# Attention beside a long convolution on one core: contiguous taps in the Toeplitz tiles, a ring of 15 exponential tiles, a shared pool of two PSUM banks, and an order that counts TensorE's changes of shape

## The chip, the cores and the metric

One NeuronCore of a Trainium2 chip (trn2). The metric is device time in microseconds (us) of one execution; lower is better.

## What is computed

The output is `g * a + (1 - g) * b` for 2048 positions and 448 channels, in bfloat16. `a` is attention with 16 query heads of 28 channels that share one key and one value head; `b` is a state-space layer, that is a causal convolution of every channel with 2048 taps of its own; `g` is one gate per position.

```python
g = sigmoid((x * gate_w).sum(-1, keepdims=True))
# a: attention
q = x @ wq                       # 16 heads of 28
k, v = x @ wk, x @ wv            # one head
p = softmax(q k^T * 28 ** -0.5)  # 16 x 2048 x 2048
a = (p v) @ wo
# b: state-space layer; A, B, C are complex, 448 x 256 states
K[d, l] = Re(sum_n C[d,n] * exp(dt[d] * A[d,n] * l) * dt[d] * B[d,n])   # l = 0..2047
y[d, t] = sum_l K[d, l] * x[t - l, d]
b = y + x * Dskip
```

## The kernel before

**A recorded program and a planner.** The kernel does not write its instruction streams by hand. Every piece of work is recorded with `Prog.op` or `Prog.dma`: its engine, the time the author assumes for it in ns, the names it reads and writes, and a priority `pr` (lower goes first). `Prog.schedule` is a list scheduler: it keeps a clock per engine, takes again and again the ready operation that can start earliest (then the lowest priority), and so fixes the order of all five engines. `Prog.emit` writes that order with semaphore waits. On the chip each engine follows its list strictly; an instruction whose input is late holds up everything behind it on that engine. The planner's constants (60 ns from one engine to another, 300 ns per DMA issue, 2200 ns from a DMA's end to its use) move nothing by themselves, but they decide the order.

**Attention.** The scores are cut into 1024 tiles of 128 keys by 512 queries: 16 groups (four query chunks times four groups of four heads) of 64 tiles each. I call such a group a head group, or head for short; its index is `i`. `qk(s)` in `main()` (L988) computes a set of alternately three and two tiles into five PSUM banks (0 to 2 and 3 to 4 of `psS`); each tile uses 29 rows of the array, so tiles of four heads lie in four row strips. One ScalarE instruction (L1001) turns the set into exponentials in `expT`, a ring of ten tiles. `pv(v)` (L1010) multiplies four tiles with `vaug` (values, and a column of ones for the denominator) into `psB`, in four column strips of 32. The lines that set the ring and its order are

```python
es = ts[0] % 10                                  # L1000, in qk(s)
... wr=[("e", t % 10) for t in ts] ...           # L1002
... rd=["va"] + [("e", t % 10) for t in ts] ...  # L1014, in pv(v)
qk(s)                                            # the loop of main()
if s >= 2:
    while nv < NTL // 4 and 4 * nv + 3 <= sets[s - 2][-1]:
        pv(nv); nv += 1
```

`norm(i)` follows a head's last product: VectorE copies `psB` to `acc` (L910), four DMAs fetch the denominators (`denT`), VectorE takes the reciprocal (L915), two more steps of DMA spread it over the partitions through `R_scratch` (`rdenB`), and L919 scales the result. `qproj(i)` makes the queries of a later head (L663, L669, L672, L675), `outp` multiplies by `wo` (L893, L902).

**The convolution.** The 448 channels go in 14 blocks of 32 (index `c`). `masters(b)` (every two blocks) and `tables(c)` build powers of `exp(dt A)` on VectorE by repeated doubling (L698 to L796); one copy of the tables is in use while the next is built. `kgen(u)` takes 16 channels: 64 matmuls (L814) give their taps, VectorE copies them from PSUM to `kstg` with the channels interleaved (L824) and adds `Dskip` to tap 0 (L827), and one DMA writes 128 pieces of 512 bytes to `KP_scratch` in DRAM. There each group of four channels is one line in which the four channels alternate, element by element.

`tload(gi)` loads one Toeplitz tile for four channels: 128 partitions of 4096 elements (8192 bytes), each partition starting one tap later than the one before; the second 64 partitions begin 1024 taps further on. Four buffers (`NTR = 4`) take turns. `conv(c)` (16 channels, 28 calls, four tiles each) multiplies each tile with the input `U`, eight groups of four matmuls, one per channel and column strip:

```python
r = e.matmul(ps.v(32 * j, 32 - 2 * n, po + 128 * k, [[1, 128]]),              # L856
             self.U.v(0, P, (4 * gi + j) * 32 + 2 * n, [[1, 32 - 2 * n]]),
             self.T.v(0, P, s * 4096 + (896 - 128 * n) * 4 + j, [[4, 128]]), ...)
```

The moving operand is thus read with a step of four elements. VectorE scales the sum (`cst`, L865), TensorE turns it round (L876), and VectorE adds it to the output tile `O` (L884). The convolution has the lowest priority of all work for TensorE.

**PSUM.** Bank 5 belongs to the sums of `conv` alone (lock `"C"`). Bank 7 (`psX`) serves everything else in turn (lock `"X"`): `qproj`, `kgen`, the turning in `conv`, `outp`, and the transposes at the start.

**Queues.** All DMAs but five loads at the start are issued by SP, in the planner's order: T loads, taps, denominators and their spreading, and the output. `tail()` finishes the last head, folds and stores.

Of the kernel before, what the change touches and what calls it, by code (L numbers as in the profile page):

```python
# [11 lines left out]
P = 128  # L12

S = 2048
# [6 lines left out]
KPW = 2112  # L21
# [9 lines left out]
NTR = 4  # L31
SIN2PI = 6.2831850
# [19 lines left out]

def dram(t, off, dims):
    return bass.AP(tensor=t.tensor, offset=t.offset + off, ap=[list(d) for d in dims])


class Op:
    __slots__ = ("i", "eng", "fn", "ns", "lat", "deps", "pr", "lock", "unlock", "slot", "ndma",
                 "count", "vc", "end", "comm", "extra")


class Prog:
    SEM_NS = 60
    DMA_NS = 2200
    SLACK = {"pe": 500.0, "dve": 300.0}
# [9 lines left out]
    def op(self, eng, fn, ns, rd=(), wr=(), pr=0, lat=60, lock=None, unlock=None, comm=None):  # L75
        o = Op()
        o.i, o.eng, o.fn, o.ns, o.lat, o.pr = len(self.ops), eng, fn, ns, lat, pr
        o.lock, o.unlock, o.slot, o.ndma = lock, unlock, None, 0
        o.comm = comm
        deps = {}  # L80
# [40 lines left out]
    def schedule(self):  # L121
# [15 lines left out]
        locks = {}  # L137
# [3 lines left out]
        while done < n:  # L141
            best = None
            for e in ENG:
                T = free[e]
                for i in ready[e]:
                    o = ops[i]
                    r = max(rt[i], T)
                    if o.lock is not None:
                        L = locks.setdefault(o.lock, [None, 0.0, []])
                        if L[0] is not None:  # L150
                            continue
                        r = max(r, L[1])
# [9 lines left out]
            ready[e].remove(i)  # L162
            if e == "pool" and o.slot is None:
                for d in reversed(order[e]):
                    if ops[d].slot is None:
                        o.deps[d] = 1
                        break
# [5 lines left out]
            if o.lock is not None:  # L173
                L = locks[o.lock]
                for d in L[2]:
                    o.deps.setdefault(d, 1)
                L[0] = o.i
                L[2] = []
            if o.slot is not None:
                free[e] = r + 300.0 * o.ndma  # L180
# [7 lines left out]
            if o.unlock is not None:  # L188
                L = locks[o.unlock]
                L[0], L[1] = None, end + self.SEM_NS  # L190
                L[2].append(i)
            for j in succ[i]:
# [4 lines left out]
                elif x.eng == e and o.slot is None:  # L197
                    t = end
# [97 lines left out]

class Kernel:
# [25 lines left out]
    def alloc(self):  # L323
# [10 lines left out]
        self.Wk = sb("Wk", NT * P, BF)  # L334
        self.Wv = sb("Wv", NT * 32, BF)
        self.Wo = sb("Wo", NT * D, BF)
        self.Wb = sb("Wb", P, BF)
        self.Wm = sb("Wm", P, BF)
        self.ident = sb("ident", P, BF)
        self.identf = sb("identf", P, F32)  # L340
        self.absq = sb("absq", 512, BF)
        self.qT = sb("qT", 2 * 512, BF)
        self.expT = sb("expT", 10 * 512, BF)
# [7 lines left out]
        self.T = sb("T", NTR * 4096, BF)  # L351
# [4 lines left out]
        self.mst = sb("mst", 2 * 2 * BW, F32)  # L356
        self.msq = sb("msq", 2 * BW, F32)
        self.msr = sb("msr", 2 * BW, F32)
        self.qst = sb("qst", 2 * BW, F32)
# [8 lines left out]
        self.KP = nc.dram_tensor("KP_scratch", (D * KPW,), BF).ap()  # L368
        self.R = nc.dram_tensor("R_scratch", (16 * 4 * 512,), F32).ap()

    def consts(self):
# [6 lines left out]
        dm(V(self.kstg, 0, 256), 0.0, 170, [("kst", 0)])  # L378
# [14 lines left out]
        for hb in range(4):  # L393
            pm(self.Wm.v(32 * hb, 28, 32 * hb + 28, [[1, 1]]), -1.0, 100, ["Wm"], 1)
        pm(V(self.identf, 0, P), 1.0, 200, ["idf"], 2)
        pg.op("pool", lambda e: e.affine_select(
            out=V(self.identf, 0, P), in_=V(self.identf, 0, P), compare_op=ALU.is_equal, fill=0.0,
            base=0, pattern=[[-1, P]], channel_multiplier=1), 300, rd=["idf"], wr=["idf"], pr=2)
# [12 lines left out]
    def loads(self):  # L411
# [56 lines left out]
        for k in range(2, 6):  # L468
            lraw(k)
        pg.dma([(self.skt.v(32 * g + 31, 1, 0, [[4, 28], [1, 4]]), dram(ins["B_Dskip"], 4 * g, [[16 * D, 1], [16, 28], [1, 4]]))  # L470
# [4 lines left out]
        pg.dma([(dram(self.KP, 4 * S, [[4 * KPW, 112], [1, 256]]), self.kstg.v(0, 112, 0, [[1, 256]]))],  # L475
               (112, 512), "pad", rd=[("kst", 0)], wr=["pad"], pr=3)
# [79 lines left out]
    def prep_gate(self):  # L556
        pg = self.pg
        X = ("gx",)
        px = self.psX
# [4 lines left out]
              rd=["og", "idf"], wr=[X], pr=2, lock="X")  # L564
# [3 lines left out]
        def mm(e):  # L568
            for mu in range(2):
# [7 lines left out]
              rd=[X], wr=["omq"], pr=2, unlock="X")  # L577

    def prep_params(self):
# [19 lines left out]
        def trans(k, bk, pr, lock=None):  # L599
            t_, o = self.bank(bk, True)  # L600
            X = ("b", bk) if bk < 7 else ("rx", k)

            def mm(e):
                for half in range(2):
                    for T in range(4):
                        r = e.matmul(t_.v(0, P, o + half * D + DT * T, [[1, DT]]),
# [3 lines left out]
            pg.op("pe", mm, 700, rd=[("raw", k), "id"], wr=[X, "rawdone"], pr=pr, lock=lock)  # L610
            return t_.v(0, P, o, [[D, 2], [1, DT], [DT, 4]]), X
# [3 lines left out]
        def vt(o, a, b, op, rd, wr, pr, **kw):  # L615
            pg.op("dve", lambda e: e.tensor_tensor(o, a, b, op), ns, rd=rd, wr=wr, pr=pr, **kw)  # L616
        p0, k0 = trans(0, 7, 0, "X")
# [474 lines left out]
```

## Time and profile before

| | |
|---|---|
| five runs | median 641.6 us (636.01 to 642.65) |
| the profiled execution | 635.38 us; span from first to last instruction 633.6 us |
| TensorE matmul / weight load busy | 528.7 us (83%) / 246.1 us (39%) |
| VectorE busy | 477.5 us (75%) |
| ScalarE busy | 495.2 us (78%), of which L1001 480.3 us |
| GpSimd busy | 21.9 us (3%) |
| mean granted TensorE clock | 0.850 |
| DMA | 133.46 MB, 211 GB/s over the span; 112 T loads of 1024 KB, median 7.9 us from issue to landing |
| largest TensorE groups | L988 183.7 us, L856 142.9 us, L1010 109.4 us, L814 85.2 us |

Busy time is the union of an engine's instructions, so overlapping matmuls count once. A line of instruction groups reads: line, engine, operation, output<-input, shapes, count, busy us and mean ns of one, idle time before them and what ended it. In the timelines a row is start (us), length (us), engine, line, operation and count, with the idle time before it and its releaser in brackets. In the table by stages a column like "17.99 (x311)" is busy us and number of instructions.

### The profile page before, as it was taken

To read this page: it belongs to the slowest core of one execution; us is meant where nothing else is said; L and a number is where in the kernel's file an instruction comes from. 1 tells how busy PE (TensorE), PEld (TensorE's weight loads), DVE (VectorE), ACT (ScalarE), POOL (GpSimd) and SP (SyncE) were. 2 spreads that over 40 slices of the span, in tenths; PEclk is the share of its full clock that TensorE was granted. 3 is DMA by queue.
4 is the path that set the end of the run, shared out by engine and by line. 5 is a ranking of instruction groups with operands and counts; after the bars stand their busy time and mean duration, and the time that the engine had idled before them with its cause. 6 is when DMAs were issued, how large, how long until landed. Compare 5 with 4: busy or idle time off the path is not lost.

```text
span 633.6 us, 18423 instructions
## 1 busy us (share of the span) xinstructions
PE 528.7 (83%) x8234; PEld 246.1 (39%) x8234; DVE 477.5 (75%) x1055; ACT 495.2 (78%) x427; POOL 21.9 (3%) x36
## 2 busy tenths in 40 slices
PE   5597878888878988788989999887988888978883
PEld 4332112343333353435444454433535342534342
DVE  7844899716999988898989999898989987211112
ACT  3689797898778878787879898877888777879760
POOL 2640000000000000000000000000000000000000
PEclk9755555697899987989989999878899885999798
DMA  8510000667934736777877567767569452598995
GB/s 253 145 46 1 19 0 3 190 212 240 377 119 155 304 107 271 281 272 279 312 251 244 209 195 300 218 255 274 209 183 341 148 182 71 159 369 314 346 396 177
DMA packets 36366, 133.46 MB, mean 211 GB/s; under 512 B 9344, under 2 KB 18736, under 8 KB 21952
## 3 DMA queue, kind: packets, MB, share of 16 engines
q1 hardware_dynamic: 35632, 131.73, 59.3%
q8 instruction: 64, 1.05, 0.7%
q10 hardware_dynamic: 656, 0.57, 0.3%
q14 instruction: 14, 0.11, 0.0%
HBM read 128.31 MB, written 3.85 MB: 209 GB/s over the span
## 4 chain that ended last, share of the span: by engine, by line
DVE 39%; PE 25%; DMA 20%; ACT 10%; SPq 4%; issue 1%; ACTq 0%
ACT expT L1001 9%; DMA denT<-acc 7%; PE psS L988 7%; DVE tab L774 6%; PE psB L1010 5%; SPq L111 4%; PE psS L856 4%; DMA R_scratch<-denT 4%; PE psX L814 4%; DMA T<-KP_scratch 4%; DMA rdenB<-R_scratch 4%; DVE tab L776 3%; DVE tab L778 2%; DVE tmp L776 2%; DVE tab L780 2%; DVE tab L791 2%
## 5 line engine op out<-in xcount | busy, mean ns | idle before, releaser
L1001 ACT ACTIVATE expT<-psS 128x1536 bf16<-128x1536 f32 (+1 forms) x410 | 480.3, 1256 | 103.7 <-PE psB L1010 67.0
L988 PE MATMUL psS<-qT,kT 29*128 29x512 bf16 x1024 | 183.7, 444 | 44.6 <-ACT expT L1001 41.8
L856 PE MATMUL psS<-T,U 128*32 128x128 bf16 (+7 forms) x3584 | 142.9, 292 | 17.9 <-DVE cst L865 13.7
L856 PEld LDWEIGHTS psS<-T,U 128*32 128x32 bf16 (+7 forms) x3584 | 89.9, 106 | 60.0 <-issue 27.4
L1010 PE MATMUL psB<-expT,vaug 128*32 128x512 bf16 x1024 | 109.4, 453 | 0.1
L988 PEld LDWEIGHTS psS<-qT,kT 29*128 29x128 bf16 x1024 | 40.3, 93 | 160.3 <-ACT expT L1001 110.6
L814 PE MATMUL psX<-tab 128*32 128x64 bf16 x1792 | 85.2, 333 | 8.5 <-DVE kstg L827 4.7
L814 PEld LDWEIGHTS psX<-tab 128*32 128x32 bf16 x1792 | 61.5, 157 | 29.3 <-issue 12.6
L774 DVE TENSOR_TENSOR tab<-tab,mbf 128x4096 bf16<-128x4096 bf16 (+4 forms) x70 | 69.7, 997 | 0.4
L1010 PEld LDWEIGHTS psB<-expT,vaug 128*32 128x32 bf16 x1024 | 22.9, 96 | 59.4 <-issue 56.8
L776 DVE TENSOR_TENSOR tmp<-tab,mbf 128x256 bf16<-128x256 bf16 (+3 forms) x56 | 37.3, 666 | 0.0
L791 DVE TENSOR_TENSOR tab<-tab,tmp 128x4096 bf16<-128x4096 bf16 x14 | 32.0, 2288 | 0.1
L776 DVE TENSOR_TENSOR tab<-tab,mbf 128x4096 bf16<-128x4096 bf16 x14 | 32.0, 2287 | 0.0
L919 DVE TENSOR_TENSOR onT<-acc,rdenB 128x512 bf16<-128x512 f32 x15 | 10.5, 701 | 27.3 <-DMA rdenB<-R_scratch 27.3
L824 DVE CAST kstg<-psX 128x256 bf16<-128x256 f32 x28 | 11.7, 418 | 21.9 <-PE psX L814 21.9
L865 DVE TENSOR_TENSOR cst<-psS,omq 128x512 bf16<-128x512 f32 x28 | 19.2, 687 | 11.7 <-PE psS L856 11.7
L698 DVE TENSOR_TENSOR msq<-mst 128x256 f32<-128x256 f32 x63 | 27.2, 431 | 0.1
L915 DVE RECIPROCAL denT<-denT 128x16 f32<-128x16 f32 x15 | 3.8, 251 | 30.9 <-DMA denT<-acc 30.9
L787 DVE TENSOR_TENSOR tmp<-tmp,mbf 128x64 bf16<-128x64 bf16 (+4 forms) x70 | 25.5, 365 | 0.6
L778 DVE TENSOR_TENSOR tab<-tab,tmp 128x128 bf16<-128x128 bf16 (+3 forms) x56 | 23.3, 415 | 0.4
L780 DVE TENSOR_TENSOR tab<-tab,tmp 128x128 bf16<-128x128 bf16 (+3 forms) x56 | 22.8, 407 | 0.0
L663 PE MATMUL psX<-xT,Wq 112*128 112x512 bf16 x64 | 21.2, 443 | 0.6 <-DVE T L616 0.3
(116 smaller groups left out, 386.5 us busy)
## 6 DMA issues: line engine op xcount, KB each, us to landing
T<-KP_scratch SPq DMA_DIRECT2D x112, 1024.0 KB, 7.9
rdenB<-R_scratch SPq DMA_DIRECT2D x60, 64.0 KB, 2.4
tab<-in_A_x_dram SPq DMA_DIRECT2D x4, 448.0 KB, 6.2
tab<-in_A_x_dram SPq DMA_DIRECT2D x16, 112.0 KB, 2.6
KP_scratch<-kstg SPq DMA_DIRECT2D x28, 64.0 KB
out_dram<-O SPq DMA_DIRECT2D x3, 448.0 KB, 3.8
denT<-acc SPq DMA_DIRECT2D x60, 2.0 KB, 3.4
tab<-in_A_x_dram SPq DMA_DIRECT2D x16, 56.0 KB, 6.9
```

What stands on the lines that cost most here:

```text
L698: pg.op("dve", lambda e, k=k: e.tensor_tensor(msq.v(0, P, 0, [[BW, 2], [1, BW]]), both(k - 1), both(k - 1), ALU.mult), el(2 * BW), rd=keys ...
L774: vo(lambda e, dst=dst, src=src, mr=mr: e.tensor_tensor(dst, src, mr, ALU.mult), 2 * n, done + mk(lv), [kr, ki])
L776: vo(lambda e, src=src, mi=mi, w=w, tb=tb, to=to: e.tensor_tensor(tb.v(0, P, to, [[w * EW, 2], [EW, w], [1, EW]]), src, mi, ALU.mult), 2 * ...
L778: vo(lambda e, do=do, n=n, tb=tb, to=to: e.tensor_tensor(tab.v(0, P, do, [[1, n]]), tab.v(0, P, do, [[1, n]]), tb.v(0, P, to + n, [[1, n]] ...
L780: vo(lambda e, do=do, n=n, tb=tb, to=to: e.tensor_tensor(tab.v(0, P, do + BLK, [[1, n]]), tab.v(0, P, do + BLK, [[1, n]]), tb.v(0, P, to, ...
L787: vo(lambda e, w=w, lv=lv: e.tensor_tensor(rho.v(0, P, (32 - 2 * w) * 64, [[64, w], [1, 64]]), rho.v(0, P, (32 - w) * 64, [[64, w], [1, 64]]),
L791: vo(lambda e: e.tensor_tensor(tab.v(0, P, FM, [[64, 2], [EW, 32], [1, 64]]), tab.v(0, P, lo + 31 * EW, [[BLK, 2], [-EW, 32], [1, 64]]), r ...
L814: r = e.matmul(self.psX.v(32 * g, 32, 64 * jj, [[1, 64]]), tab.v(0, P, lo + comp * BLK + 64 + o, [[EW, 32]]), tab.v(0, P, fo, [[mo - fo, 2 ...
L856: r = e.matmul(ps.v(32 * j, 32 - 2 * n, po + 128 * k, [[1, 128]]), self.U.v(0, P, (4 * gi + j) * 32 + 2 * n, [[1, 32 - 2 * n]]), self.T.v( ...
L988: r = e.matmul(self.psS.v(0, P, 512 * (bo + k), [[1, 512]]), kT.v(32 * h, DH + 1, 128 * kt, [[1, 128]]), qT.v(32 * h, DH + 1, 512 * (i % 2 ...
L1001: pg.op("act", lambda e: e.activation(expT.v(0, P, 512 * es, [[1, n]]), self.psS.v(0, P, 512 * bo, [[1, n]]), AF.Exp, scale=SQ), 100 + n / ...
L1010: r = e.matmul(self.psB.v(32 * h, 32, 0, [[1, 512]]), vaug.v(0, P, 32 * kt, [[1, 32]]), expT.v(0, P, 512 * (t % 10), [[1, 512]]), start=(k ...
```

## The change

1. **Taps as two padded halves.** `KP_scratch` holds two halves of one row per channel: taps 0 to 1087 in the first, 1024 on in the second (`KW = 1088`). `kgen` takes a whole block of 32 channels at once and copies the taps without interleaving; eight DMAs write them, for each of four groups of eight channels one of 17 and one of 16 rows of eight 128-byte pieces. A T tile is now 3 x 1088 + 1024 = 4288 elements per partition, the four channels one after another, and L893 (L856 before) reads its 128 columns with a step of one.
2. **Ring of 15.** `expT` has 15 tiles. To make room, small weights live in its last two tiles until they are used, and `absq`, `identf`, `msr` and the second halves of `mst` and `qst` share other buffers or go.
3. **Bank pool.** Banks 7 and 5 form one pool; each group of work (`grp()`) takes whichever the planner finds free.
4. **The planner.** It adds 105 ns when TensorE goes from one shape class to another (`mode`: scores "q", column strips "c", turning "h", full "f"), uses new delays between engines, 500 ns per DMA issue, and new assumed durations. The order of all engines changes with it.
5. **Small moves.** The start-up exponentials and sines get priority -1; the last `norm` and its identity matrix are declared after the convolution; one tail product uses the pool.

The core of the diff:

```diff
-KPW = 2112
+RING = 15
+KW = 1088
+KH = D * KW
+TW = 3 * KW + 1024
...
+    LAT = {"pe": 165.0, "act": 70.0, "dve": 85.0, "pool": 85.0, "sp": 60.0}
+    SAME = {"act": 100.0, "dve": 125.0, "pool": 150.0}
+    SWITCH = 105.0
+    POOL = (7, 5)
...
-        locks = {}
+        locks = [[None, 0.0, [], b] for b in self.POOL]
+        mode = None
...
-                        L = locks.setdefault(o.lock, [None, 0.0, []])
-                        if L[0] is not None:
+                        L = min((x for x in locks if x[0] is None), key=lambda x: x[1], default=None)
+                        if L is None:
                             continue
...
+            if e == "pe" and o.mode != mode:
+                r = max(r, free[e] + self.SWITCH)
+                mode = o.mode
...
-                free[e] = r + 300.0 * o.ndma
+                free[e] = r + 500.0 * o.ndma
...
-        self.expT = sb("expT", 10 * 512, BF)
+        self.expT = sb("expT", RING * 512, BF)
...
-        self.T = sb("T", NTR * 4096, BF)
+        self.T = sb("T", NTR * TW, BF)
...
-        self.mst = sb("mst", 2 * 2 * BW, F32)
+        self.mst = sb("mst", 2 * BW, F32)
-        self.qst = sb("qst", 2 * BW, F32)
+        self.qst = sb("qst", BW, F32)
...
-    def kgen(self, u):
+    def kgen(self, c):
...
-        for jj in range(4):
+        for jj in range(8):
...
-        pg.op("dve", lambda e: e.tensor_copy(self.kstg.v(0, P, ks * 256, [[4, 64], [1, 4]]),
-                                             self.psX.v(0, P, 0, [[1, 64], [64, 4]])),
-              el(256), rd=[X], wr=[("kst", ks)], pr=2)
...
+        pg.op("dve", lambda e: e.tensor_copy(self.kstg.v(0, P, 0, [[64, 8], [1, 63]]), G.v(0, P, 0, [[64, 8], [1, 63]])),
+              el(504), rd=[X], wr=["kst2"], pr=2, unlock=G)
-        pg.dma([(dram(self.KP, u * 16 * KPW, [[4 * KPW, 4], [256, 32], [1, 256]]),
-                 self.kstg.v(0, P, ks * 256, [[1, 256]]))],
-               (128, 512), f"kw{ks}", rd=[("kst", ks)], wr=[("KP", u)], pr=0)
+        lst = []
+        for g in range(4):
+            for h, (r0, nr) in enumerate(((0, 17), (16, 16))):
+                lst.append((dram(self.KP, h * KH + (32 * c + 8 * g) * KW, [[64, nr], [KW, 8], [1, 64]]),
+                            self.kstg.v(32 * g + r0, nr, 0, [[64, 8], [1, 64]])))
+        pg.dma(lst, (1056, 128), "kw", rd=["kst", "kst2"], wr=[("KP", c)], pr=0)
...
-        pg.dma([(self.T.v(0, P, s * 4096, [[1, 4096]]),
-                 dram(self.KP, 4 * gi * KPW, [[4, 64], [4096, 2], [1, 4096]]))],
-               (128, 8192), f"T{s}", rd=[("KP", gi // 4), "pad"], wr=w, pr=1, extra=3000)
+        pg.dma([(self.T.v(0, P, s * TW, [[1, TW]]),
+                 dram(self.KP, 4 * gi * KW, [[1, 64], [KH, 2], [1, TW]]))],
+               (128, 2 * TW), f"T{s}", rd=[("KP", gi // 8), "pad"] + x, wr=[("T", s)], pr=1, extra=1500)
...
-        ps, po = self.bank(5)
-        px = self.psX
+        ps, px = self.grp(), self.grp()
...
-                                     self.T.v(0, P, s * 4096 + (896 - 128 * n) * 4 + j, [[4, 128]]),
+                                     self.T.v(0, P, s * TW + j * KW + 896 - 128 * n, [[1, 128]]),
...
-                pg.op("pe", mm, 125, rd=[("T", s)] + [("U", q) for q in range(4)],
+                pg.op("pe", mm, 70, mode="c", rd=[("T", s)] + [("U", q) for q in range(4)],
...
-            pg.op("pe", mm, 330, rd=sorted(rd, key=str), wr=bk, pr=0)
+            pg.op("pe", mm, 220, rd=sorted(rd, key=str), wr=bk, pr=0, mode="q")
-            es = ts[0] % 10
+            es = ts[0] % RING
...
-            pg.op("pe", mm, 250, rd=["va"] + [("e", t % 10) for t in ts], wr=[("b", 6)], pr=0.5)
+            pg.op("pe", mm, 230, rd=["va"] + [("e", t % RING) for t in ts], wr=[("b", 6)], pr=0.5, mode="c")
```

## The prediction

> **What bounds the kernel now.** I read ScalarE's waits first, since its exponentials (L1001: 410 instructions, 480.3 us) are the longest single job; then ScalarE's timeline, the table by stages, TensorE's timeline and the DMA view. The waits, with the columns total us, times, longest:
>
> ```profile
> ACT expT L1001 <- PE psB L1010: 67.0, 53, 4.4
> ACT expT L1001 <- PE psS L988: 34.6, 52, 2.2
> ```
>
> Between its first exponential at 29.4 us and the end of its last at 612.9 us ScalarE stands still for about 103 us. Two thirds of that is one event that returns, as its timeline shows (start, length, form of the first, number of instructions, idle before):
>
> ```profile
> 82.71 3.76 ACT L1001 ACTIVATE expT<-psS 128x1536 bf16<-128x1536 f32 x3
> 87.73 9.14 ACT L1001 ACTIVATE expT<-psS 128x1024 bf16<-128x1024 f32 x8 [1.27 <-PE psB L1010]
> 98.14 2.37 ACT L1001 ACTIVATE expT<-psS 128x1024 bf16<-128x1024 f32 x2 [1.26 <-PE psB L1010]
> ```
>
> Eight exponentials run without a gap, then 1.26 us are lost before a two-tile one. Eight sets are 20 tiles. The value product (L1010) takes four tiles at a time, the ring refills five, so once in 20 tiles a group straddles: it shares its first ring slot with the exponential just issued, waits for it, and the next exponential, which refills the group's other slots, waits for the group. I call this the seam.
>
> The stages show that no engine is far from being the bound in the middle, and that the end is another regime:
>
> ```profile
> core 0: us, PE busy (x) PEld busy (x) DVE busy (x) ACT busy (x) POOL busy (x), PEclk, DMA share, GB/s
> 420.00:440.00 20.00, 17.99 (x311) 8.91 (x307) 16.76 (x40) 16.52 (x15) 0.00 (x0) 0.92 0.68 236
> ...
> 560.00:580.00 20.00, 15.81 (x316) 7.60 (x318) 2.83 (x5) 16.96 (x16) 0.00 (x0) 1.00 0.97 352
> ```
>
> At 420 us TensorE, VectorE and ScalarE are each over 80% busy; at 560 us VectorE has finished its tables, and the DMA engines are 97% busy with the T loads. TensorE's timeline gives the marks of the two regimes (first block's taps done, last block's taps done, last T load used):
>
> ```profile
> 115.48 0.48 PE L814 MATMUL psX<-tab 128*32 128x64 bf16 x8
> 545.67 0.50 PE L814 MATMUL psX<-tab 128*32 128x64 bf16 x8
> 622.09 1.12 PE L856 MATMUL psS<-T,U 128*32 128x128 bf16 x32 [0.64 <-DMA T<-KP_scratch]
> ```
>
> So the time is: start to 116.0; 13 more blocks of 32 channels to 546.2, or 33.1 us each; then the convolutions left over, 27 of 112 T loads, to 622.1, 26 gaps of 2.92 us; then 11.5 us to the end of the span at 633.6. The profiled execution took 635.4, 1.8 more; the median of the five runs, 641.6, is 1% above it.
>
> **Ring of 15: the seam goes.** The listing of TensorE's order has 752 score tiles between the marks of blocks 0 and 13. At 480.3/1024 = 0.469 us a tile ScalarE works 352.7 of those 430.2 us and idles 77.5, 5.96 per block. A seam every 20 tiles is 37.6 x 1.26 = 47.4 us, 3.65 per block; 2.3 per block are other waits, mostly for scores behind background work. With 15 slots the slots that an exponential refills belong to groups that are declared at least a set earlier, and three to four exponentials lie between. I take the whole 3.65 off. The cover that remains is thin: the order of the changed kernel has 797 tiles between the marks (123 before block 0, 920 before block 13), 61.3 per block, 28.75 us of exponentials; with 2.3 of other waits, 31.05.
>
> **VectorE under it.** Its busy time from 120 to 540 us in the table by stages is 366 us, 28.2 per block, 28.5 with the stretch from 116. The taps' copies fall from two of 0.42 and two of 0.16 (L824, L827) to one of each at 512 columns (0.68 by L675's cast) and 8: minus 0.3. Buffers that lose their second half (mst, qst) raise VectorE's waits on itself from 403 to 477 instructions, 5 per block; at up to 0.1 us, plus 0.5. So 28.7 per block. What it waits for in the middle is the softmax's denominator chain: 30.9 us (L915) and 27.3 us (L919) in 15 heads, 3.7 per block if it stays, which gives 32.4. The planner now counts 500 ns per DMA issue instead of 300 (a denT issue takes 0.59 us), so these instructions stand later in the order; I take a pace of 31.4, nearer to ScalarE's 31.05 than to 32.4.
>
> **Contiguous taps: TensorE's convolution.** The rows that price it, all at full clock:
>
> ```profile
> 617.75 0.42 PE L856 MATMUL psS<-T,U 128*30 128x128 bf16 x8
> 618.80 2.65 PE L856 MATMUL psS<-T,U 128*26 128x128 bf16 x84
> 617.28 0.45 PE L876 MATMUL psX<-ident,cst 128*64 128x64 bf16 x16
> 299.62 0.40 PE L1010 MATMUL psB<-expT,vaug 128*32 128x512 bf16 x4
> 304.87 0.62 PE L1010 MATMUL psB<-expT,vaug 128*32 128x512 bf16 x8
> ```
>
> 76 more convolution matmuls cost 2.23 us: 29.3 ns each, 117 per group of four that read 128 columns with a step of 8 bytes. Four L1010 matmuls read 512 columns without a step in 0.22 us, so 128 would take 55. L876 fits sixteen loads and matmuls in 0.45 us, so loading does not hold a group above 65 to 80. Bounds 55 and 117; I take 65. The order has 80 T loads used between the marks, 6.2 per block, 8 groups each: 49 x 52 ns = 2.6 us of TensorE per block. TensorE is 365 of 420 us busy from 120 to 540, 28.8 per block; plus 3.5 tiles more per block at 0.19 us, minus 2.6, is 26.9 of 31.4. This saves nothing on the path by itself: ScalarE and VectorE cover it. Without it TensorE would need 29.5 and would be a third bound.
>
> The Trainium skill speaks against this part. "SBUF — State Buffer", section "Door 1: The DMA port swizzle", says that reads keep full bandwidth when two accesses fall into a 16-byte line, so that bf16 may be strided by up to 8 elements for free; a step of four would cost nothing and the convolution would stay at 117. L856 against L1010 contradicts it, 117 against 55; by the rule the sum is that of the third case below.
>
> **Writing the taps.** Two writes of 128 pieces of 512 B per block become eight with 1056 pieces of 128 B, four of them with 17 rows. SP issues them at 0.59 us each: 4.7 instead of 1.2 per block; behind them in SP's queue stand T loads and the denominators' DMAs, late by up to 3.5 us, which the ring of four T buffers hides (TensorE waited 10.4 us in all for T). The DMA view of 1.1 us around one write of today:
>
> ```profile
> DMA packets 132, 0.07 MB, mean 60 GB/s; under 512 B 4, under 2 KB 132, under 8 KB 132
> q1 hardware_dynamic: 132, 0.07, 21.4%
> ```
>
> 21.4% of 16 engines in 1.1 us is 3.8 us for 128 packets, some 28 ns each, within 0.9 us: about four engines at work. Around a 64 B write the same view has 11.6% in 0.8 us for 144 packets, 10.4 ns each. So a 128 B piece costs between 10.4 and 28 ns, 13 by size. Spread over 16 engines a block's pieces cost 0.9 us. If the 17-row writes each fall on one engine, 544 pieces cost 7 us there (5.7 to 15). Six T loads put 6.2 x 3 = 19 us on every engine, so at 13 ns this fits into 31.4 and I add nothing.
>
> The skill's "DMA: Bandwidth & Descriptors", section "Why a DMA increments its semaphore by 16 and not by 1", says that a DMA uses the largest number of engines up to 16 that divides its outermost dimensions. Today's write has 4 outermost and shows four engines, as the rule has it; 17 would give one. The sum by the rule is mine at 13 ns and the fourth case at 28.
>
> **The order, the pool, the start.** Counted in the listings, TensorE changes shape 844 times before and 856 after; that the planner now charges for it saves nothing. The pool lets a convolution start while VectorE still reads the last (L856 waited 31.7 us for that in 21 times), worth 0 to 2.3 us of TensorE per block, which is not the bound: 0. Block 0 comes after 123 tiles instead of 153: 29.4 + 123 x 0.469 is 87 for ScalarE, but VectorE finished block 0's tables only at 99.6 (L796), with about 19 us idle between 20 and 60 that the earlier seeds can fill partly. I take 102 for the mark, bounds 92 and 112.
>
> **The tail grows.** Block 13 ends after 80 T loads are used instead of 85. A load grows from 8192 to 8576 B per partition, so 2.92 becomes 3.06; 31 gaps are 95, plus 11.5: 106 instead of 87.
>
> **Sum.** 102 + 13 x 31.4 = 510; plus 106 = 616 for the span, 618 for the execution, 17 below 635.4. The median lies 6.2 above this execution, and I add half: 621.
>
> **Rivals.** (1) Forecast, 55%: 607 to 640 (mark 98 and pace 30.9 to mark 108 and pace 32.4, and the 3 us of the median). (2) The queues mesh better, 20%: VectorE's waits halve, the pace is 30 and T loads come at 379 GB/s, the best 20 us of the trace (2.9 each): 97 + 390 + 90 + 11.5 + 2 = 590. For it: every cost in the planner is now nearer to the rows; against: three engines within 5% of each other. (3) The layout does not do what it says, 13%: groups stay at 117 (or 100, if loading 32 columns holds them), TensorE needs 29.5 per block and its waits return; pace 33.2: 102 + 432 + 106 + 2 = 642. Against it stands L1010. (4) Slower, 12%: the 17-row writes sit on one DMA engine at 28 ns a piece, 15.2 us per block. With T loads 18.5 and 1 for the rest that engine needs 34.7 per block, each T load waits for its slowest engine, TensorE holds the scores behind it: 102 + 451 + 106 + 2 = 661. It decides from 22 ns a piece on (12 us per block). For it the one row of 512 B; against it the 64 B row.
>
> **How the numbers follow.** Faster by over 1% (below 635, about what a measurement of this kernel can tell from no change): most of the first case and all of the second, 0.67. Within 1%: the upper end of the first and most of the third, 0.18. Slower: the fourth and what is left, 0.15. The range, 597 to 648, leaves out half of the second case and the fourth; the first case alone spans 607 to 640.
>
> **What would show it.** Right: ScalarE's wait for L1010 falls below 15 us; convolution matmuls come every 14 to 20 ns; block 13's taps end near 510; 106 us remain, with DMA over 90%. Wrong: marks more than 33 us apart, T loads landing later than 12 us in the middle (the fourth case), convolution matmuls still at 29 ns (the third), or a granted clock well under today's 0.85, since a lighter TensorE might be throttled more.

## The result, and the profile after

The changed kernel takes 643.5 us (median), the kernel before 639.0 in the same sessions: a ratio of 1.0073, 95% interval 1.0058 to 1.0088, so 0.7% slower. The forecast was 621 us, and faster. The profiled execution of the changed kernel has a span of 640.0 us (633.6 before). Times here and below are medians of all executions of a kernel; ratios leave out the few executions that fell into a slower state.

Its table by stages, in the two windows that the prediction shows of the kernel before (busy us and number of instructions, granted clock, DMA share, GB/s):

```profile
core 0: us, PE busy (x) PEld busy (x) DVE busy (x) ACT busy (x) POOL busy (x), PEclk, DMA share, GB/s
420.00:440.00 20.00, 19.57 (x384) 9.64 (x386) 17.62 (x47) 18.24 (x17) 0.00 (x0) 0.75 0.80 307
560.00:580.00 20.00, 14.49 (x345) 6.50 (x344) 1.81 (x5) 19.84 (x18) 0.00 (x0) 1.00 1.01 390
```

The marks, from TensorE's timeline: last taps of block 0, last taps of block 13, last T load used:

```profile
91.40 0.39 PE L851 MATMUL psX<-tab 128*32 128x64 bf16 x8
532.68 0.87 PE L851 MATMUL psX<-tab 128*32 128x64 bf16 x24
629.54 1.04 PE L893 MATMUL psX<-T,U 128*32 128x128 bf16 x32 [1.50 <-DMA T<-KP_scratch]
```

So block 0 is done at 91.8 instead of 116.0 (24.2 us won), 13 blocks take 441.8 instead of 430.2 (11.6 lost; 34.0 us each, which I call the pace), and the rest takes 106.5 instead of 87.5 (19.0 lost). That is the 6.4 us of the span.

The waits of ScalarE, VectorE and TensorE (total us, times, longest):

```profile
ACT expT L1047 <- PE psS L1031: 84.8, 82, 4.8
...
DVE denT L952 <- DMA denT<-acc: 59.8, 14, 8.1
...
PE psX L893 <- DMA T<-KP_scratch: 24.6, 13, 4.2
...
PE psS L893 <- DMA T<-KP_scratch: 14.9, 12, 3.3
```

The last three have these counterparts in the kernel before (there the convolution writes to one bank only):

```profile
DVE denT L915 <- DMA denT<-acc: 30.9, 13, 5.6
...
PE psS L856 <- DMA T<-KP_scratch: 4.1, 6, 1.0
```

The seam is gone: no wait of ScalarE for the value product is left (67.0 us before). But it now waits 84.8 us for scores (34.6 before), VectorE 59.8 for denominators (30.9), and TensorE's matmuls 24.6 + 14.9 = 39.5 for T (4.1). Two of the three are waits for DMAs. SP's own timeline shows what stands in their way (start, length, number of issues):

```profile
230.19 11.42 SPq L128 DMA_DIRECT2D KP_scratch<-kstg  x8
241.66 1.17 SPq L128 DMA_DIRECT2D T<-KP_scratch  x2
242.87 2.52 SPq L128 DMA_DIRECT2D denT<-acc  x4
```

For 11.4 us, the longest of the 14 blocks, SP does nothing but issue one block's eight writes of taps; two T loads and a head's denominators stand behind them. In the trace a 17-row issue takes 0.29 us, but the 16-row issue right behind it takes 1.3 us in the median and up to 6.05. Over the run the writes hold SP for 102 us, 7.3 per block. In the semaphores' events a block's eight writes count 72: 16 for each 16-row write and 2 for each 17-row one. (Two single copies in the experiments below, hot_engine's of 17 rows and spread_copy's of 16, count 2 and 16 in the same way; the write before the change, with about four engines at work, counts 5, so below 16 one event is not an engine's.) So a 16-row write runs on 16 DMA engines and a 17-row write on one. This is what the Trainium skill says in "DMA: Bandwidth & Descriptors", section "Why a DMA increments its semaphore by 16 and not by 1": the number of engines is the largest, up to 16, that divides the slowest dimension of both access patterns. The DMA view of half a microsecond (96.0 to 96.5 us) in which a 17-row write runs:

```profile
DMA packets 51, 0.01 MB, mean 13 GB/s; under 512 B 51, under 2 KB 51, under 8 KB 51
q1 hardware_dynamic: 51, 0.01, 9.1%
```

9.1% of 16 engines in 0.5 us is 0.73 us for 51 pieces: 14 ns each, between one and two engines at work.

### The profile page after: what moved, and what is told of

Its sections match the earlier page's. It is cut to its first block, busy times and chain, and to the rows that moved or that the text cites. A ratio compares the mean times of both kernels' runs of the same rounds, so it can differ in the third digit from the quotient of the medians.

```text
span 640.0 us, 18475 instructions
## 1 busy us (share of the span) xinstructions
PE 507.6 (79%) x8234; PEld 220.4 (34%) x8234; DVE 471.3 (74%) x1028; ACT 489.1 (76%) x427; POOL 23.7 (4%) x36
## 4 chain that ended last, share of the span: by engine, by line
DMA 34%; DVE 31%; PE 18%; ACT 8%; SPq 6%; issue 2%; ACTq 0%
DMA denT<-acc 15%; ACT expT L1047 8%; DMA R_scratch<-denT 7%; DMA T<-KP_scratch 6%; SPq L128 6%; PE psS L1031 6%; DVE tab L812 4%; DMA rdenB<-R_scratch 4%; PE psB L1056 4%; DVE tab L816 2%; DVE tab L818 2%; DVE tmp L814 2%; PE psX L893 2%; DVE tab L814 2%; DVE msq L736 1%
## 5 line engine op out<-in xcount | busy, mean ns | idle before, releaser
L1047 ACT ACTIVATE expT<-psS 128x1536 bf16<-128x1536 f32 (+1 forms) x410 | 474.2, 1270 | 86.7 <-PE psS L1031 84.8
L1031 PE MATMUL psS<-qT,kT 29*128 29x512 bf16 x1024 | 196.2, 476 | 31.6 <-ACT expT L1047 29.5
L1056 PE MATMUL psB<-expT,vaug 128*32 128x512 bf16 x1024 | 125.3, 480 | 0.0
L893 PE MATMUL psX<-T,U 128*18 128x128 bf16 (+7 forms) x1792 | 49.8, 261 | 34.8 <-DMA T<-KP_scratch 24.6
L812 DVE TENSOR_TENSOR tab<-tab,mbf 128x256 bf16<-128x256 bf16 (+4 forms) x70 | 68.7, 982 | 0.3
L893 PE MATMUL psS<-T,U 128*18 128x128 bf16 (+7 forms) x1792 | 51.0, 255 | 19.3 <-DMA T<-KP_scratch 14.9
L893 PEld LDWEIGHTS psX<-T,U 128*18 128x18 bf16 (+7 forms) x1792 | 35.7, 111 | 53.1 <-DMA T<-KP_scratch 29.5
L851 PE MATMUL psX<-tab 128*32 128x64 bf16 x1280 | 50.7, 289 | 2.9 <-DVE tab L834 2.9
L893 PEld LDWEIGHTS psS<-T,U 128*18 128x18 bf16 (+7 forms) x1792 | 34.8, 107 | 39.9 <-DMA T<-KP_scratch 18.2
L952 DVE RECIPROCAL denT<-denT 128x16 f32<-128x16 f32 x15 | 3.8, 252 | 59.8 <-DMA denT<-acc 59.8
L851 PEld LDWEIGHTS psX<-tab 128*32 128x32 bf16 x1280 | 36.8, 137 | 18.5 <-issue 12.1
L956 DVE TENSOR_TENSOR onT<-acc,rdenB 128x512 bf16<-128x512 f32 x15 | 10.3, 690 | 17.8 <-DMA rdenB<-R_scratch 17.8
L816 DVE TENSOR_TENSOR tab<-tab,tmp 128x128 bf16<-128x128 bf16 (+3 forms) x56 | 22.7, 405 | 0.2
```

The lines of the kernel that those rows point to most:

```text
L812: vo(lambda e, dst=dst, src=src, mr=mr: e.tensor_tensor(dst, src, mr, ALU.mult), 2 * n, done + mk(lv), [kr, ki])
L816: vo(lambda e, do=do, n=n, tb=tb, to=to: e.tensor_tensor(tab.v(0, P, do, [[1, n]]), tab.v(0, P, do, [[1, n]]), tb.v(0, P, to + n, [[1, n]] ...
L851: r = e.matmul(G.v(32 * g, 32, 64 * jj, [[1, 64]]), tab.v(0, P, lo + comp * BLK + 64 + o, [[EW, 32]]), tab.v(0, P, fo, [[mo - fo, 2], [EW, ...
L893: r = e.matmul(ps.v(32 * j, 32 - 2 * n, 128 * k, [[1, 128]]), self.U.v(0, P, (4 * gi + j) * 32 + 2 * n, [[1, 32 - 2 * n]]), self.T.v(0, P, ...
L1031: r = e.matmul(self.psS.v(0, P, 512 * (bo + k), [[1, 512]]), kT.v(32 * h, DH + 1, 128 * kt, [[1, 128]]), qT.v(32 * h, DH + 1, 512 * (i % 2 ...
L1047: pg.op("act", lambda e: e.activation(expT.v(0, P, 512 * es, [[1, n]]), self.psS.v(0, P, 512 * bo, [[1, n]]), AF.Exp, scale=SQ), 100 + n / ...
```

## The experiments

All kernels were planned by the same scheduler. "The same order" means that every engine's list is unchanged but for the DMAs named. Marks and pace are read from each kernel's TensorE timeline as above; the ratio is to the kernel before. The first theories were: A, the 17-row writes sit on one DMA engine and what is queued behind them comes late; B, the new plan asks for T and denominators without a margin; C, the denominators wait in one queue behind up to four T loads.

| kernel | time, us | ratio (95%) | block 0 done | us per block | rest after block 13 | T loads in the rest |
|---|---|---|---|---|---|---|
| changed kernel | 643.5 | 1.0073 (1.0058 to 1.0088) | 91.8 | 34.0 | 106.5 | 31.8 |
| even_rows | 615.4 | 0.9635 (0.9582 to 0.9688) | 91.1 | 32.0 | 104.5 | 31.8 |
| sp_hold | 643.0 | 1.0090 (1.0045 to 1.0135) | 91.1 | 33.8 | 108.5 | 31.8 |
| hot_engine | 656.4 | 1.0276 (1.0192 to 1.0360) | 91.9 | 34.7 | 111.1 | 31.8 |
| spread_copy | 621.9 | 0.9736 (0.9667 to 0.9806) | 93.3 | 32.1 | 105.5 | 31.8 |
| step_four | 612.5 | 0.9599 (0.9543 to 0.9656) | 91.7 | 31.8 | 105.8 | 31.8 |
| one_denominator_dma | 600.6 | 0.9401 (0.9353 to 0.9449) | 90.9 | 31.2 | 103.0 | 31.8 |
| even_no_switch | 588.1 | 0.9195 (0.9135 to 0.9254) | 90.3 | 33.1 | 62.7 | 15.6 |

### The first four: pieces, plan, ring, queue

**even_rows** cuts the same taps into eight writes of 16 rows and one of 4 x 8 pieces; the planner still counts eight issues, so the order is the same:

```diff
-        lst = []
+        lst = [(dram(self.KP, 32 * c * KW + 1024, [[8 * KW, 4], [KW, 8], [1, 64]]), self.row16())]
...
-            for h, (r0, nr) in enumerate(((0, 17), (16, 16))):
+            for h, (r0, nr) in enumerate(((0, 16), (16, 16))):
```

> The taps' write of the changed kernel, cut into eight DMAs of 16 rows and one of 4 x 8 pieces for row 16, in place of four of 17 and four of 16 rows; every other instruction of every engine is in the same order. Theory A (the 17-row DMAs sit on one DMA engine, SP is held at the next issue, and T loads and denominators behind them come late): SP's issues of 16-row pieces fall from a median of 1.3 us to 0.6, a block's taps land within 6 us of their first issue instead of 8 to 12.5, TensorE's waits for T fall from 39.5 us to under 20, ScalarE's for scores from 84.8 to under 65, and the time is 622 to 634. Theory B (the order asks for T and denominators too early, whatever the pieces): the writes land sooner but the waits stay within 10%, and the time is 639 to 646.

Measured: 615.4 us, 28 less, from one row fewer in each of four writes. SP's timeline for the same block, and the waits:

```profile
220.68 5.06 SPq L128 DMA_DIRECT2D KP_scratch<-kstg  x9
```

```profile
ACT expT L1047 <- PE psS L1031: 57.7, 75, 3.1
...
DVE denT L952 <- DMA denT<-acc: 32.8, 13, 7.3
...
PE psX L893 <- DMA T<-KP_scratch: 14.5, 12, 1.6
...
PE psS L893 <- DMA T<-KP_scratch: 4.8, 6, 1.9
```

Nine issues take 5.1 us instead of 11.4 for eight; over the run 4.8 per block instead of 7.3. Waits for scores fall by 27 us, for denominators by 27, for T from 39.5 to 19.3. Theory A holds against B. Three of its numbers missed: the time is 6.6 us below its range, a 16-row issue takes 0.43 us and not 0.6, and a block's taps still land 5.8 to 9.5 us after the first issue, not within 6.

**extra_3000** edits one number of the plan:

```diff
-               ... pr=1, extra=1500)
+               ... pr=1, extra=3000)
```

> The changed kernel planned with 3000 ns instead of 1500 as the assumed time from a T load's end to its use, as before the change; nothing else is edited, but all orders are planned anew. Theory B (with 1500 the plan leaves T loads no margin): TensorE's waits for T fall from 39.5 us to 10 to 20, ScalarE's waits for scores from 84.8 to under 70, time 628 to 637. Theory A (single-engine writes): T still lands late, waits for T stay over 30 us, time 639 to 647.

Measured: 649.8 us, ratio 1.0174 (1.0115 to 1.0233), above both ranges. TensorE's matmuls still wait 34.8 us for T. A larger margin in the plan doesn't help; theory B falls again.

**ring_10** plans the changed kernel with the old ring of ten tiles:

```diff
-RING = 15
+RING = 10
```

> The changed kernel with a ring of 10 exponential tiles; planned anew. If the ring's seam costs what the prediction said, 3.65 us per block come back: ScalarE waits some 50 us or more for the value product, and the time rises by 25 to 48 us, to 668 to 691. If the middle is bound by what TensorE and VectorE wait for, the seam is covered by those waits: ScalarE's waits for scores fall as those for the value product rise, and the time stays within 12 us of 643.

Measured: 660.5 us, ratio 1.0326 (1.0265 to 1.0388), 17 more than with 15, below the lower end of the first expectation and above the second. ScalarE's wait for the value product is back (73.9 us), that for scores falls to 60.8.

**pool_queue** gives the denominators' nine DMAs to GpSimd:

```diff
-                   (128, 64), "dn", rd=["acc"], wr=["dn"], pr=0)
+                   (128, 64), "dn", rd=["acc"], wr=["dn"], pr=0, eng="pool")
```

> The changed kernel with the nine DMAs of a head's denominators issued by GpSimd instead of SP, so that they no longer stand behind T loads and taps in SP's queue. Theory C (denominators wait in one queue behind up to four T loads, VectorE stands still for them, tables and scores come late): denominators land in 3 to 6 us instead of a mean of 9, VectorE's wait for them falls from 59.8 us to under 30, time 625 to 636. Theories A and B: VectorE's wait falls too, but TensorE's waits for T stay at some 40 us and the time within 5 us of 643; if GpSimd's own issues are slow (over 1 us each), the chain gets longer and the time is over 646.

Measured: 629.0 us, ratio 0.9842 (0.9776 to 0.9909), inside the range of C, but not for C's reason ("rw" and "rdb" are edited in the same way). VectorE's wait for denominators falls to 32.0, yet its wait for the spread reciprocals rises from 17.8 to 39.5; TensorE's matmuls still wait 35.0 for T. The pace is 33.8, hardly better; the rest after block 13 shrinks by 6.8, with 26.8 T loads left there by the new plan. So this run gives C little.

### What the 17 rows cost: SP's time or one engine's

All four are the kernel with even rows in the same order. **hot_engine**, **spread_copy** and **sp_hold** add one operation after each block's taps:

```diff
+    lst = [(dram(self.HX, c * 17 * 4096, [[4096, 17], [1, 4096]]), self.U.v(0, 17, 0, [[1, 4096]]))]   # hot_engine; 16 rows: spread_copy
+    lst = [(dram(self.HX, (c * 5 + k) * 1024, [[64, 16], [1, 64]]), self.U.v(0, 16, 64 * k, [[1, 64]])) for k in range(5)]   # sp_hold
+    self.pg.dma(lst, (0, 128), "hx", rd=["kst", "kst2"] + [("U", q) for q in range(4)], wr=[("HX", c)], pr=0)
```

> Base: the kernel with even rows (615.4 us). After each block's taps one more DMA copies 17 rows of 8192 bytes of the input tile to an unused place in DRAM: 17 pieces that fall on one DMA engine, by the T loads' 0.324 us per 8576 bytes some 5.3 us of that engine per block, for one short issue on SP. All other orders are unchanged. Theory A1 (the changed kernel loses its time because one DMA engine is behind and every T load and denominator waits for its share there): the loss comes back, 635 to 646. Theory A2 (it loses because SP is held while it issues the 17-row pieces): the time stays within 4 us of 615.

Measured: 656.4 us, ratio 1.0276, 10 above the range of A1 and far from that of A2. The copy lands 6.6 to 7.8 us after its issue.

> The control of the run before: the same extra copy with 16 rows of 8192 bytes, which spread over 16 DMA engines, 0.3 us each. Both theories: 613 to 619. If it costs as much as the 17-row copy, the extra bytes or the extra issue count, not the single engine.

Measured: 621.9 us, ratio 0.9736, 3 above the expected range: bytes and the extra issue cost 6.4 us. The copy lands 2.6 to 3.8 us after its issue. The single engine therefore costs 656.4 - 621.9 = 34.5 us, with what it does to SP: over the run SP's issues take 255.3 us in hot_engine and 242.5 in spread_copy, so a part of the 34.5 may be SP's.

> Base: the kernel with even rows. After each block's taps SP issues five more DMAs of 16 pieces of 128 bytes to an unused place in DRAM: some 2.5 us of SP per block, which is what the 17-row form costs SP more than the even form (7.3 against 4.8 us of issues per block), and hardly any work for the DMA engines. Theory A2 (SP held): 632 to 646. Theory A1 (one DMA engine behind): within 5 us of 615.

Measured: 643.0 us, ratio 1.0090. The five issues take 2.5 us per block, as the 17-row form takes more than the even one. The waits are those of the changed kernel, one by one (84.8, 59.8, 24.6 and 14.9 there):

```profile
ACT expT L1047 <- PE psS L1031: 83.9, 88, 4.8
...
DVE denT L952 <- DMA denT<-acc: 57.2, 14, 9.6
...
PE psX L893 <- DMA T<-KP_scratch: 23.7, 14, 4.9
...
PE psS L893 <- DMA T<-KP_scratch: 17.1, 8, 4.1
```

So both mechanisms can make a loss of this size: A1 and A2 each told half. SP's lost time, put back alone, gives the changed kernel's time, pace and waits; that is enough to explain it. A single engine 5 us behind costs as much by another road: in hot_engine the waits for T reach 56.7 us, and a T load lands 9.7 us after its issue (median; 8.7 in spread_copy). The changed kernel shows neither: 39.5 us, and 8.7 us (8.9 with even rows). So the road through SP is the likely one; a share of the single engine's lag isn't excluded. Whether SP is held because that one engine's queue is full was not tried.

**step_four** reads the convolution's columns with the old step:

```diff
-  self.T.v(0, P, s * TW + j * KW + 896 - 128 * n, [[1, 128]]),
+  self.T.v(0, P, s * TW + j * KW + 512 - 64 * n, [[4, 128]]),
```

> Base: the kernel with even rows, but the convolution reads its 128 columns of the T tile with a step of four elements, as before the change; it reads other columns than it should, so the convolution is changed, and only the time counts. All orders are unchanged. If the layout only takes work off TensorE that others cover, as the prediction said: 612 to 622, with convolution matmuls at 29 ns. If TensorE becomes a third bound (the third case of the prediction, about 2.6 us per block more on TensorE): 628 to 650.

Measured: 612.5 us, ratio 0.9599, not slower than with contiguous columns (615.4). TensorE's timelines, eight and 32 convolution matmuls each, of the changed kernel and then of step_four:

```profile
563.18 0.63 PE L893 MATMUL psS<-T,U 128*32 128x128 bf16 x32 [0.50 <-DMA T<-KP_scratch]
...
568.53 0.30 PE L893 MATMUL psS<-T,U 128*32 128x128 bf16 x8 [0.82 <-DMA T<-KP_scratch]
```

```profile
261.02 1.10 PE L893 MATMUL psS<-T,U 128*32 128x128 bf16 x32
...
265.63 0.40 PE L893 MATMUL psS<-T,U 128*32 128x128 bf16 x8
```

(0.63 - 0.30) / 24 is 14 ns a matmul, (1.10 - 0.40) / 24 is 29, both at a granted clock of 1.00 in these microseconds: the layout does what it says. It just buys no time. One reason stands in the clock, which the cores' views give for even_rows and for step_four, and in the rows of the score matmuls, which are the same instructions in both (busy us, mean ns of one):

```profile
core 0: 611.4 us, clock 0.753
```

```profile
L1031 PE MATMUL psS<-qT,kT 29*128 29x512 bf16 x1024 | 196.7, 476 | 43.3 <-ACT expT L1047 36.5 <-DVE qT L707 4.0 <-issue 0.8
```

```profile
core 0: 610.8 us, clock 0.850
```

```profile
L1031 PE MATMUL psS<-qT,kT 29*128 29x512 bf16 x1024 | 180.0, 435 | 35.4 <-ACT expT L1047 28.0 <-DVE qT L707 4.6 <-issue 0.7
```

The lighter TensorE is granted less (0.753) and the heavier as much as before the change (0.850). The convolution's matmuls are busy for 34 us less in even_rows (99.4 against 133.5), but the scores take 16.7 us more and the value products 9.6 more (124.9 against 115.3), so TensorE's whole busy time falls only from 504.7 to 501.3 us. The colder clock gives back most of what the layout wins on TensorE. No run here has the short convolution at the warm clock; what the layout would be worth there is open.

### Ring, plan and SP with even rows

> The kernel with even rows and a ring of 10 exponential tiles, planned anew: what the ring is worth once the taps' write holds nobody up. The prediction's term is 3.65 us in each of 13 blocks and some 2 more blocks' worth of tiles outside the marks: 615 plus 47 to 55, 662 to 670. If the waits for scores cover half of the seam, as between the first pair of runs (660.5 against 643.5): 630 to 642.

The edit is RING = 10 in the kernel with even rows. Measured: 635.1 us, ratio 0.9935 (0.9894 to 0.9976), in the second range; the ring, with the plan that it allows, is worth 20 us. The exponentials end at 622.3 us instead of 562.4, 60 us later, more than the seam's 47. But with the small ring the convolutions are done at 591, before the exponentials; with the large one they last to 602, 40 us behind them. Most of what the ring gives to ScalarE is given back in the tail.

**even_no_switch** plans without the price of a shape change:

```diff
-    SWITCH = 105.0
+    SWITCH = 0.0
```

> The kernel with even rows, planned without the 105 ns for a change of TensorE's shape. If the term buys nothing, as the prediction said: 609 to 622. If the order it makes is what holds the pace: over 625.

Measured: 588.1 us, ratio 0.9195: both expectations miss. The order explains it: 96 T loads instead of 80 are used before block 13's taps are done, and all 112 before the last value product (97 with the price). The middle slows by 1.1 us per block, and the rest falls from 104.5 to 62.7 us. TensorE changes shape 823 times in this order, 856 times in the one that pays for changes: the price saved none and only pushed convolutions to the end.

**one_denominator_dma** fetches a head's denominators with one DMA instead of four, in the same order:

```diff
-  pg.dma([(self.denT.v(32 * h, 32, ...), self.acc.v(32 * h + 28, 1, ...)) for h in range(4)],
+  pg.dma([(self.denT.v(0, P, 0, [[1, 16]]), bass.AP(tensor=self.acc.h, offset=28 * self.acc.rs, ap=[[32 * self.acc.rs, 4], [16, 32], [1, 16]]))],
```

> The kernel with even rows, and the four DMAs that fetch a head's denominators made one; the order of all engines is unchanged. SP spends some 28 us less on issues in the whole run, 1.9 per head. If SP's time is what holds the middle at the price of the run with five more issues per block (34.5 us of SP made 27.5 us): 593 to 607. If SP is no longer in the way at this point and only the latency of the denominators counts: 608 to 614. If one DMA on fewer engines lands later: 616 or more.

Measured: 600.6 us, ratio 0.9401, in the first range; the middle falls to 31.2 us per block. Some 28 us less of SP are worth 15 us: SP's time still counts, at two thirds of sp_hold's price (0.53 against 0.80 us for each us of SP). VectorE's wait for denominators falls from 32.8 to 17.6 us; how much of that comes from SP's time and how much from a head's denominators standing in one issue, this run doesn't tell.

**taps_on_gpsimd** adds `eng="pool"` to the taps' DMA.

> The kernel with even rows, the nine DMAs of a block's taps issued by GpSimd, which is idle in the middle, in place of SP; planned anew, since SP's and GpSimd's lists change. SP spends 4.8 us less per block. At the price above, 0.8 us for each us of SP: 560 to 580, which ScalarE's floor cannot give; with ScalarE's 28.75 us per block and 1.5 of other waits, 91 + 393 + 104 + 2: 585 to 600. If GpSimd's DMAs land later or the order gets worse: 610 to 630.

Measured: 591.3 us, ratio 0.9281 (0.9224 to 0.9338), 31.4 us per block and a rest of 86.7 with 25.6 T loads. The SP theory's range by the full price was far too low, the one with ScalarE's floor right; part of the gain is the new order, which has six T loads fewer at the end.

### The price of a shape change in the changed kernel itself, and what remains

> The changed kernel as it is, with its 17-row writes, planned without the 105 ns for a change of shape. In its order 96 T loads instead of 80 are used before the last block's taps are done, and all 112 before the last value product; TensorE changes shape 823 times instead of 856. If the price costs its time through the tail whatever the writes do: the pace of the middle rises from 34.0 us per block to 34.5 to 35.5, the tail falls from 106 to 60 to 70, and the time is 613 to 622. If the held SP queue takes the gain back, because 16 more T loads stand in it in the middle: 630 to 645.

SWITCH = 0 in the changed kernel. Measured: 627.1 us, ratio 0.9806 (0.9774 to 0.9838), between the two ranges. The middle slows to 35.4 us per block and the rest falls to some 73. So the price costs the changed kernel 16 us, less than with even rows. A likely reason is that the 16 more T loads have to pass the held SP in the middle: VectorE waits 74.4 us for denominators here, and 44.7 in even_no_switch.

> Even rows, no price for a change of shape, and the denominators of a head in one DMA. If the two gains on the kernel with even rows (27 and 15 us) add up: 571 to 576. If ScalarE's own work now decides (476 us of exponentials, 30 us before the first, some 12 after the last, and 60 of waits): 578 to 585.

Measured: 585.8 us, ratio 0.9103 (0.9028 to 0.9178). The gains do not add. The median is 0.8 us above the second range, the ratio makes 581 us of the 638.3 that the kernel before took beside it: ScalarE's own work, the second expectation, fits; the sum of the gains doesn't.

> The same with the taps' DMAs issued by GpSimd, which leaves SP 4.8 us more per block. If SP's time still counts: 555 to 568. If it has gone off the path: within 5 us of the run before.

Measured: 588.2 us, ratio 0.9207 (0.9167 to 0.9247), within 5 us of the run before: with these orders, SP has left the path. Both beat the kernel before by 8 to 9%, and neither is told apart from even_no_switch. In all three the last exponential ends at 571 or 572 us; ScalarE's exponentials and some 62 us of waits for scores are what is left.

No run separates the rest of the change: the bank pool, the new delays and the 500 ns per issue in the planner, and the small moves.

## Why the prediction was wrong, step by step

- **The step that failed** is "Writing the taps", at two sentences: that T loads and denominators would be "late by up to 3.5 us, which the ring of four T buffers hides", and that 7 us on one engine "fits into 31.4 and I add nothing". It was priced at 0 and was worth 28 us: with it gone the same order takes 615.4. One engine and 13 ns a piece were right (14 measured). Two things were wrong. The writes took 7.3 us of SP per block, not 4.7. (Even 4.7 would not have been free: with even rows they take 4.8, and 28 us less of SP's issues in one_denominator_dma still gained 15.) And I compared busy time with the length of a block. What counts is how long the queue's next entries stand: hot_engine loses 34.5 us with an engine that has room, and sp_hold loses 27.5 us for 2.5 us of SP per block. That TensorE waited so little for T before the change did not mean that there was cover: sp_hold brings these waits from 19.3 to 40.8 us, and VectorE's for denominators from 32.8 to 57.2. The prediction's 10.4 us adds the matmuls' wait (4.1) to that of the weight loads before them (6.3), as its 31.7 for the pool adds 13.7 and 18.0; the matmuls' alone is what stands against 39.5.
- **The fourth case** named the place (one engine), but asked for 22 ns a piece before it would count. The loss came at 14 ns, most likely through SP. It is neither the forecast's zero nor that case's 661. The 643.5 us lie inside the stated range, 597 to 648, but for neither of the reasons that the prediction had for its upper end (block 0 done at 108 and a pace of 32.4 in the first case, a convolution still at 29 ns in the third).
- **The pace** of 31.4 was nearly right without that term: 32.0 with even rows. That 615.4 comes near the forecast's 621 is luck in part: the first block comes 11 us sooner than forecast, and 0.6 us in each of 13 blocks takes back 8. In the changed kernel, too, the start's 10 us hid a third of the 34 us that the middle lost against the forecast.
- **The order**: "saves nothing" is wrong in sign. The 105 ns per shape change cost 16 us in the changed kernel and 27 with even rows. I counted the changes (844 and 856) and the T loads left over in the same listing and did not join the two: the fewer loads used in the middle were the price's work (80 with it, 96 without).
- **The tail** was forecast as 106 and measured as 106.5, by two errors that cancel. The last eight T loads come 2.59 us apart (611.41 to 629.54 on TensorE's timeline), not 3.06: eight packets of 0.324 us fill an engine for 2.59. The older gaps were longer than their packets too (eight of 0.309 us are 2.47, counted were 2.92), so they had waits in them. But the DMA engines were 80% busy at 540 to 560 and 78% at 580 to 600, while the last exponentials were still running, up to 590.6 us.
- **The ring**: the seam is gone and the exponentials end 60 us sooner for it, but the time gains 20, because the tail was taken as fixed while everything before it moved.
- **The layout**: 14 ns in the forecast's range of 14 to 20, and worth nothing in time, as said. But the reason given, that ScalarE and VectorE cover TensorE, isn't shown, since the colder clock took back 26 of its 34 us on TensorE. The third case, in which a step that stays at 29 ns costs 642 us, is refuted by step_four. The skill's rule in "SBUF — State Buffer", section "Door 1: The DMA port swizzle", that such a step is free, disagrees with the measured 29 against 14 ns.
- **The start** came at 91.8, the lower bound: VectorE is 99% busy from 40 to 100 us. **The clock** fell to 0.756 as feared. In time it is set off by the shorter convolution, as step_four shows.

## What to carry to other kernels

Price a DMA by the time that its queue stands for it, the issuing engine's included, and ask what is behind it in that queue; a share of busy time, even a low one, is no cover. Look at the row count of every DMA that is cut by hand: 16 rows and one row apart cost 28 us less here than 17. When a planner is given a new price, count whether it gets less of what it pays for, and look at what it pushes to the end. When work is taken off TensorE, compare an instruction that was not changed (here the scores, 435 and 476 ns): a lower granted clock can take the gain back.

## What the hardware did that was not expected

- An issue of a 16-row write takes SP 0.43 us in the median when its neighbours run on 16 engines, and 1.3 us, at most 6.05, when it follows a write of 136 pieces on one engine.
- One extra copy of 17 rows per block on a single DMA engine, which the T loads fill about half (6.2 loads of 2.59 us in 32 us), made the kernel 34.5 us slower than a copy of 16 rows spread over 16 engines.
- TensorE was granted 0.753 of full clock with the shorter convolution and 0.850 with the longer one, in an otherwise equal order and at nearly the same time (0.753 to 0.770 and 0.849 to 0.862 over four executions each). A score matmul took 476 and 435 ns.
